# Weight gradient matmuls between the output gradient steps of chunk 1, gradient loads in two parts, and a home of its own for the second half of the attention rows

## The chip, the cores and the metric

The kernel runs on one core of a Trainium2 chip, in one launch. The metric is the device time in microseconds, the median of several runs. A core has TensorE (PE in the profile; its weight loads stand as PEld), VectorE (DVE), ScalarE (ACT), GpSimd (POOL) and SyncE (SP). All five run their own instruction streams in order and meet through semaphores. Transfers run on 16 DMA engines; this kernel issues them from three places: SP (queue q1 in the profile), ACT (q10) and POOL (q0, which has the indirect gathers too).

## The reference: what is computed

One transformer block, forward and backward: the output `h2` and the gradients with respect to the input and six of the weights.

```python
def _A_ref(x, wqkv, wo):            # B, S, D = 1, 2048, 512; H = 32; Dh = 16; W, dil = 8, 2
    ...                             # q, k, v = x @ wqkv, by head
    off = jnp.arange(W) * dil       # each position sees itself and 7 earlier ones, 2 apart
    ...
    attn = _softmax(logits, axis=-1)
    o = jnp.einsum("bhsw,bhswd->bhsd", attn, vg)
    return (...)(o, 0, 2, 1, 3).reshape(B, S, D) @ wo

def _B_ref(x, w1, b1, w2, b2):      # F = 1792
    h = _gelu(jnp.einsum("bsd,df->bsf", x, w1) + b1)
    return jnp.einsum("bsf,fd->bsd", h, w2) + b2

h = x + _A_ref(_layernorm(x, axis=-1), A_wqkv, A_wo)
h2 = h + _B_ref(_layernorm(h, axis=-1), B_w1, B_b1, B_w2, B_b2)
...
_out, _vjp = jax.vjp(_f, A_x, A_wqkv, A_wo, B_w1, B_b1, B_w2, B_b2)
return (_out0, *[jnp.asarray(_g) for _g in _vjp(grad_out)])
```

All arrays are bf16. The attention has no matmul form of the usual kind: each query has eight keys, so its products are made on VectorE over gathered rows and summed on TensorE with small constant matrices.

## The kernel before

The 2048 tokens are worked in four chunks of 512 (`NC = 4`), each of four tiles of 128 tokens. There are three parts in time.

1. Forward attention for all chunks, and the second layer norm.
2. Forward and backward MLP by chunk. It writes the activations and their gradients, turned into rows of tokens, to two DRAM tensors: `gT_d` (gelu output) and `ghT_d` (gradient before gelu). `gh_all[c]` is the gradient with respect to `h`. The loads of the output gradient (`gout_r`, two tiles of 1 MB) for part three are issued from ACT here. A scheduler sets the order of parts one and two.
3. Backward attention. From `tc.manual_schedule()` (L817) on, every engine has its instructions in exactly the order in which the Python code emits them.

In part three two strands are woven together by hand. The **main strand** loops over the chunks (L1100). For chunk `c` it makes the softmax gradient (`ga_prod` on DVE, L656; `ga_sum` on PE, L662), and then three kinds of "band": for the gradients of q (chunk `c`), of v and of k (chunk `c-1`). A band (`band_tile`, L1004) takes a tile of gathered rows `R` (an indirect gather from POOL, L224), multiplies it on DVE by coefficients (`prb`, L1012), sums on PE (`ps_band`, L1026), is copied by ACT to `gqs` or `gks` (L1029) and stored by POOL to the DRAM tensors `g3_d` (`gq_d`, `gk_d`, `gv_d`, L1031). `p3_go(c)` (L1040) makes the gradient of the attention output of chunk `c` in four steps: `a` transposes `gh_all[c]` (L162, copied by ACT at L163 to `ghT`), two steps `b` multiply it by `woT` (L646, copied at L647 to `got`, through one PSUM tile `psL` with a single buffer), and `t` turns it into rows (L210), which ACT copies (`tmst`, L213) and SP stores to `go_d` (L215, L219). The gathers for the v bands read `go_d`.

The **filler strand** is the weight gradients, a generator `wgrads()` (L891): seven pairs of columns for `w2` (`ps_gw`, L896), seven for `w1` (L904), then `wo` (L914) and `wqkv` in the order q, v, k (L924). One matmul is 128x512 wide (128x256 for `w1`). Results leave PSUM through a two-bank pool `psF`, an ACT copy to `gwst` (L831) and a store from ACT (L833).

Work that is due later stands in a list `pend` with the number of slots until then (`later`, L968); `slot(dve_us)` (L971) emits what is due, and then fills with filler matmuls up to `RATIO = 1.4` times the DVE time given, less the PE time just emitted. `filler(us)` (L947) adds its argument to a running debt and draws matmuls, each paid with its cost (`MM = 0.22`), while the debt is positive; a generator can also yield a letter, a gate, at which it stops until the main strand has opened it.

Just ahead of the loop, chunk 1's output gradient is made in one go:

```python
    load_ln1(0)
    load_R()
    load_R()
    p3_go(1, (1, 1, 1, 1))
    slot(0.0)
```

Loads of the filler strand are issued from SP, in the order in which the code emits them, among the main strand's stores. `load_t` (L751) brings one pair of columns of `gT_d` or `ghT_d` (`gwm`, 1 MB, 8 KB in a row per partition) into one of two homes; the load for pair `q + 2` is emitted when pair `q` is done. `load_half` (L738) brings half of the 2048 token rows of a tensor (1 MB, rows of 1 KB) into one of three homes (`rtile`, L734): two are old weight tiles, the third (`r8`, k = 2) is shared by the first half of the layer norm rows `ln2_r` and the second half of the attention rows `o_r`, whose load therefore waits until the first half of the last `w1` pair is computed. `load_g3` (L850) brings one half (1 MB) of `g3_d` into `gqh`. `load_perm` (L841) brings the `ln1_r` rows in eight small loads. SP stands still at a load whose home is not free, and everything emitted behind it stands too.

`shift` (L1058) copies coefficients between partitions: four ACT copies (`sh`, L1062), each emitted after a number of slots given by `at`; the k and v bands need all four (through a DVE transpose to `cf`, L246).

Of the kernel before, what the change touches and what calls it, by code (L numbers as in the profile page):

```python
# [10 lines left out]
P = 128  # L11
BF16 = mybir.dt.bfloat16
# [24 lines left out]
def kernel(  # L37
# [21 lines left out]
    V, A, T, G, SY = nc.vector, nc.scalar, nc.tensor, nc.gpsimd, nc.sync  # L59
# [4 lines left out]
    S, D = xf.shape  # L64
# [3 lines left out]
    NC = S // CH  # L68
# [224 lines left out]
    wff = LP("wff")  # L293
# [444 lines left out]
    def load_half(name, src, i, k, eng=None):  # L738
        r = rtile(name, k)
        n = NT // 2  # L740
        (eng or SY).dma_start(out=r[:], in_=src[i * n * P:(i + 1) * n * P, :].rearrange("(t p) d -> p t d", p=P))
        return r

    ngm = [0]
# [5 lines left out]

    def load_t(src, q, eng=None):  # L751
        t_ = mtile("gwm", [P, 2, NT, P])
        (eng or SY).dma_start(out=t_[:].rearrange("p a t f -> p (a t f)"),
                              in_=src[:, 2 * q:2 * q + 2].rearrange("p a c n -> p (a c n)"))
        return t_

    gout_r = []
# [66 lines left out]
    HN = NT // 2  # L824
    MM = 0.22

    def wg_sink(dst_ap, width=D):
        st = pt3("gwst")

        def sink(o, ps):  # L830
            A.copy(out=st[:, o, :], in_=ps[:])  # L831
            if sink.n:
                A.dma_start(out=dst_ap, in_=st[:].rearrange("p a (b d) -> p (a b) d", d=width))  # L833
            sink.n += 1
        sink.n = 0
        return sink

    def wrows(dst, r0, n, c0, width):
        return dst[r0:r0 + n * P, c0:c0 + width].rearrange("(a p) d -> p a d", p=P)

    def load_perm(name, src, i, k):  # L841
        r = rtile(name, k)
        for j in range(4):
            for m in range(2):
                r0 = i * HN * P + 4 * m + j
                SY.dma_start(out=r[32 * j:32 * j + 32].rearrange("p (s m) d -> p s m d", m=2)[:, :, m, :],
                             in_=_ap(src[r0:r0 + 1, :], [[8 * D, 32], [256 * D, HN // 2], [1, D]]))
        return r

    def load_g3(sel, i):  # L850
        if sel == 2:
            t_ = pt3("rows", "gqh")[:, 0:HN, :]
        else:
            t_ = mtile("gqh", [P, HN, D])
        SY.dma_start(out=t_[:], in_=g3_d[sel][:, i * HN:(i + 1) * HN, :])
        return t_

    def mm_pair(name, mm, cost, sink, sub=1, by_half=False, mid=None):
# [31 lines left out]

    def wgrads():  # L891
        ln2_r = [load_half("ln2_r", ln2_d, 0, 2)]
        o_r = []
        for q in range(7):
            g_ = tiles[q]
            yield from mm_pair("ps_gw2", lambda ps, o, u, i, t, k: T.matmul(ps[:], lhsT=g_[:, o, i * HN + t, :], rhs=gout_r[i][:, t, :], **k), MM,  # L896
                               wg_sink(wrows(out_6, 2 * q * P, 2, 0, D)), by_half=(q == 6),
                               mid=(lambda: ln2_r.append(load_half("ln2_r", ln2_d, 1, 0))) if q == 6 else None)
            n = q + 2
            tiles.append(load_t(gT_d, n) if n < 7 else load_t(ghT_d, n - 7))  # L900
        o_r.append(load_half("o_r", o_d, 0, 1))
        for q in range(7):
            g_ = tiles[7 + q]
            yield from mm_pair("ps_gw1", lambda ps, o, u, i, t, k: T.matmul(  # L904
                ps[:, 256 * u:256 * u + 256].rearrange("p (a f) -> p a f", a=2),
                lhsT=ln2_r[i][:, t, (2 * o + u) * P:(2 * o + u + 1) * P], rhs=g_[:, :, i * HN + t, :], **k), MM / 2,
                wg_sink(wrows(out_4, 0, 4, q * 256, 256), 256), sub=2, by_half=q in (0, 6),
                mid=(lambda: o_r.append(load_half("o_r", o_d, 1, 2))) if q == 6 else None)
            if q + 2 < 7:
                tiles.append(load_t(ghT_d, q + 2))  # L910
        want.append(("q", 0))
        ln1_r = [load_perm("ln1_r", ln1_d, 0, 0)]
        for k2 in range(2):
            yield from mm_pair("ps_gwo", lambda ps, o, u, i, t, k: T.matmul(  # L914
                ps[:], lhsT=o_r[i][:, t, (2 * k2 + o) * P:(2 * k2 + o + 1) * P],
                rhs=gh_all[(i * HN + t) // TPC][:, (i * HN + t) % TPC, :], **k), MM,
                wg_sink(wrows(out_3, 2 * k2 * P, 2, 0, D)), by_half=True,
                mid=(lambda: ln1_r.append(load_perm("ln1_r", ln1_d, 1, 1))) if k2 == 1 else None)
        for si, sel in enumerate((0, 2, 1)):
            yield "qvk"[si]  # L920
            if sel not in hv:
                fetch(sel)
            for d2 in range(2):
                yield from mm_pair("ps_gwq", lambda ps, o, u, i, t, k: T.matmul(  # L924
                    ps[:], lhsT=ln1_r[i][:, t, (2 * d2 + o) * P:(2 * d2 + o + 1) * P], rhs=hv[sel][i][:, t, :], **k), MM,
                    wg_sink(wrows(out_2, 2 * d2 * P, 2, sel * D, D)), by_half=(si == 0 and d2 == 0))
            if sel == 0:
                want.append(("k", 1))

    hv = {}  # L930
    want = [("v", 2)]
# [39 lines left out]
    def slot(dve_us):  # L971
        pe = 0.0
        for x in list(pend):
            x[0] -= 1
            if x[0] <= 0:
                pend.remove(x)
                x[2]()
                pe += x[1]
        filler(dve_us * RATIO - pe)
# [60 lines left out]
    def p3_go(c, at=(1, 2, 3, 4)):  # L1040
        ghT = pt3("ghT")
        got = pt3("got")
        st3[c]["got"] = got

        def a():
            to_fm(gh_all[c], ghT)

        def b(g0):
            def f():
                go_pair(g0, ghT, got)  # L1050
            return f

        def t():
            to_tm_store(p3, got, 0, go_d, c, False, stage=lambda: pt3("tmst"))
        for n, cost, f in zip(at, (1.0, 1.8, 1.8, 1.0), (a, b(0), b(2), t)):
            later(n, cost, f)

    def shift(c, src, at):  # L1058
        sh = pt3("sh")

        def cp(w4):
            A.copy(out=sh[32 * w4:32 * w4 + 32],  # L1062
                   in_=_sub(src[32 * w4:32 * w4 + 32, 0, 0:1], [[SP + 2, 2], [1, 512]], c * CH + 4 * w4))
        for w4 in range(4):
            later(at[w4], 0.0, lambda w4=w4: cp(w4))
        return sh
# [28 lines left out]
    load_ln1(0)  # L1095
    load_R()
    load_R()
    p3_go(1, (1, 1, 1, 1))
    slot(0.0)
    for c in range(NC + 2):  # L1100
        if 0 < c < NC:
            got, vw = st3[c]["got"], st3[c]["vw"]
# [31 lines left out]
                      lambda gs=gs, sc=sc, c=c: unperm(gs[:], gqkv[c - 1][:, 8:12, :], 4, sc * 256))  # L1134

        if c == NC:
            shk = shift(c - 1, glf, (1, 1, 2, 2))
        if c > 0:
            vtile(0)
            vtile(1)  # L1140
# [7 lines left out]
        if 0 < c < NC:  # L1148
            V.tensor_tensor(out=glf[:, :, c * CH:(c + 1) * CH], in0=L[:], in1=attn_c(c), op=ALU.mult)
            if c == 1:  # L1150
                V.memset(glf[:, :, S:SP], 0.0)
        if c < NC:
            cfq = coefs(pt3, glf[:, 0, 0:1], c * CH, SP)
        if 0 < c < NC:
# [82 lines left out]
```

## Time and profile before

| | before |
|---|---|
| median of 5 runs | 668.12 us (665.82 to 671.17) |
| the profiled execution: its time | 666.55 us |
| its span, first to last instruction | 664.4 us |
| PE busy in the span | 597.0 us, 90% |
| DVE busy | 517.3 us, 78% |
| ACT busy | 375.9 us, 57% |
| POOL busy | 149.5 us, 22% |
| moved by DMA | 158.98 MB, 239 GB/s in the mean |
| part three, first transposes for chunk 1 | at 377.9 us |

Busy time is the union of an engine's instructions. Times in the views are from the start of the span. In a timeline row the bracket tells how long the engine stood idle before the row, and whose end released it; in the rows of windows the columns are the stretch, its length, the busy time of PE, PEld, DVE, ACT and POOL (instructions in brackets), the granted TensorE clock as a share of full speed, the DMA engines' busy share, and GB/s.

### The profile page before, as it was taken

To read this page: it belongs to the slowest core of one execution; us is meant where nothing else is said; L and a number is where in the kernel's file an instruction comes from. 1 tells how busy PE (TensorE), PEld (TensorE's weight loads), DVE (VectorE), ACT (ScalarE), POOL (GpSimd) and SP (SyncE) were. 2 spreads that over 40 slices of the span, in tenths; PEclk is the share of its full clock that TensorE was granted. 3 is DMA by queue.
4 is the path that set the end of the run, shared out by engine and by line. 5 is a ranking of instruction groups with operands and counts; after the bars stand their busy time and mean duration, and the time that the engine had idled before them with its cause. 6 is when DMAs were issued, how large, how long until landed. Compare 5 with 4: busy or idle time off the path is not lost. (4 is left out here: it accounts for less than half of the span.)

```text
span 664.4 us, 10165 instructions
## 1 busy us (share of the span) xinstructions
PE 597.0 (90%) x3854; PEld 290.1 (44%) x3916; DVE 517.3 (78%) x760; ACT 375.9 (57%) x601; POOL 149.5 (22%) x183
## 2 busy tenths in 40 slices
PE   3888989697699899999999979989999999979897
PEld 1443434332344344444444433434566667434343
DVE  7989979868899668888849768867977789569230
ACT  2587877688684567377351353684368337455321
POOL 3341535431101111110110222221232023112010
PEclk9999999898899989999999989999999999999999
DMA  8583849744999995987995999887797679997621
GB/s 277 172 290 119 294 146 299 245 137 96 218 224 254 229 259 126 239 237 170 252 279 165 282 330 343 340 275 286 238 396 287 247 231 340 356 308 255 210 77 47
DMA packets 147947, 158.98 MB, mean 239 GB/s; under 512 B 94476, under 2 KB 132540, under 8 KB 141244
## 3 DMA queue, kind: packets, MB, share of 16 engines
q1 hardware_dynamic: 120076, 69.58, 41.4%
q0 software_dynamic: 15376, 77.63, 33.7%
q10 hardware_dynamic: 12448, 11.14, 5.3%
q8 instruction: 30, 0.49, 0.3%
q14 instruction: 17, 0.14, 0.1%
HBM read 87.76 MB, written 48.03 MB: 204 GB/s over the span
## 5 line engine op out<-in xcount | busy, mean ns | idle before, releaser
L1012 DVE TENSOR_TENSOR prb<-R,cf 128x2048 bf16<-128x2048 bf16 x96 | 111.5, 1220 | 28.5 <-PE ps_band L1026 21.6
L184 ACT ACTIVATE gyr<-ps_gl,rstd 128x512 bf16<-128x512 f32 x32 | 22.0, 687 | 86.1 <-PE ps_gl L636 48.8
L577 PE MATMUL ps_h<-ln2T,w 128*128 128x512 bf16 x217 | 56.7, 386 | 3.8 <-ACT xa L579 3.1
L610 PE MATMUL ps_f<-w,gt 128*128 128x512 bf16 x219 | 53.4, 393 | 4.2 <-DVE gt L585 3.9
L896 PE MATMUL ps_gw<-gout_r,gwm 128*128 128x512 bf16 x216 | 51.8, 385 | 3.2 <-DMA gwm<-gT_d 2.2
L622 PE MATMUL ps_gg<-goT,w2T 128*128 128x512 bf16 x220 | 54.1, 378 | 0.4
L904 PE MATMUL ps_gw<-gwm,ln_r 128*128 128x256 bf16 x448 | 52.9, 273 | 0.7 <-ACT gwst L831 0.7
L636 PE MATMUL ps_gl<-w1T,dt 128*128 128x512 bf16 x219 | 51.7, 379 | 0.8 <-ACT gyr L184 0.4
L924 PE MATMUL ps_gwq<-gqh,ln_r 128*128 128x512 bf16 x186 | 44.2, 386 | 6.3 <-ACT gwst L831 3.7
L341 PE MATMUL ps_qkv<-ln1T,wqkv 128*128 128x512 bf16 x185 | 46.9, 392 | 1.0 <-DMA go_d<-zrow 0.6
L656 DVE TENSOR_TENSOR pr<-got,vw 128x4096 bf16<-128x4096 bf16 x16 | 36.2, 2287 | 14.9 <-ACT got L653 9.7
L904 PEld LDWEIGHTS <-ln_r 128*128 128x128 bf16 x448 | 43.0, 98 | 9.2 <-issue 3.0
L578 ACT ACTIVATE xb<-ps_h,b1c 128x512 bf16<-128x512 f32 x56 | 38.3, 693 | 12.0 <-DVE xa L589 6.5
L624 DVE CUSTOM_DVE_ANT_0 dt<-ps_gg,dt 128x512 bf16<-128x512 f32 x56 | 37.6, 685 | 8.5 <-PE ps_gg L622 8.4
L579 ACT ACTIVATE xa<-ps_h,b1c 128x512 bf16<-128x512 f32 x56 | 38.3, 699 | 9.5 <-DVE dt L590 9.5
L562 POOL DMA_DIRECT2D gT_d<-tst x16 | 12.4, 774 | 133.9 <-DMA tst<-gt 132.0
L280 ACT COPY gqkvT<-ptu 128x1024 bf16<-128x1024 bf16 x24 | 24.3, 1011 | 28.9 <-PE ptu L279 28.8
L262 DVE TENSOR_TENSOR prb<-R,cf 128x2048 bf16<-128x2048 bf16 x32 | 37.6, 1210 | 2.9 <-DMA R<-v_d,rowi 1.9
L232 DVE TENSOR_TENSOR pr<-qt,kt 128x4096 bf16<-128x4096 bf16 x16 | 36.1, 2286 | 2.1 <-PE ps_band L267 1.1
L610 PEld LDWEIGHTS <-gt 128*128 128x128 bf16 x224 | 22.5, 101 | 33.0 <-DVE gt L585 4.9
L213 ACT COPY tmst<-ptm 128x1024 bf16<-128x1024 bf16 x32 | 31.3, 1022 | 6.4 <-PE ptm L210 3.7
L636 PEld LDWEIGHTS <-dt 128*128 128x128 bf16 x224 | 21.4, 98 | 29.0 <-DVE gb1p L624 2.4
(182 smaller groups left out, 1130.0 us busy)
## 6 DMA issues: line engine op xcount, KB each, us to landing
gwm<-ghT_d SPq DMA_DIRECT2D x7, 1024.0 KB
gT_d<-tst POOLq DMA_DIRECT2D x12, 512.0 KB
ghT_d<-tst POOLq DMA_DIRECT2D x12, 512.0 KB
gwm<-gT_d SPq DMA_DIRECT2D x6, 1024.0 KB
out_dram<-gwst ACTq DMA_DIRECT2D x22, 256.0 KB
ln_d<-ln POOLq DMA_DIRECT2D x8, 512.0 KB
vw<-vf_d SPq DMA_DIRECT2D x4, 528.0 KB
xt<-in_A_x_dram SPq DMA_DIRECT2D x4, 512.0 KB
```

Source lines behind the costliest of these rows:

```text
L262: V.tensor_tensor(out=pr[:, hf].rearrange("p j (d h) -> p j d h", h=H), in0=R[:, o:o + 4, :].rearrange("p j (d h) -> p j d h", h=H), in1=c ...
L341: T.matmul(ps[:], lhsT=wqkv[:, dc, sel * D + g * P:sel * D + (g + 1) * P], rhs=st_[c]["ln1T"][:, dc, :], start=(dc == 0), stop=(dc == DC - 1))
L577: T.matmul(ps[:], lhsT=wcol(w1, dc, f), rhs=ln2T[c][:, dc, :], start=(dc == 0), stop=(dc == DC - 1))
L578: A.activation(out=xb[:, f - f0, :], in_=ps[:], func=ACT.Identity, bias=b1c[:, f:f + 1])
L579: A.activation(out=x2[:, f - f0, :], in_=ps[:], func=ACT.Square, bias=b1c[:, f:f + 1])
L610: T.matmul(ps[:], lhsT=gts[f // 4][:, f % 4, j * P:(j + 1) * P], rhs=wrow(w2, f), start=(f == 0), stop=False)
L622: T.matmul(ps[:], lhsT=wcol(w2T, dc, f), rhs=goT[:, dc, :], start=(dc == 0), stop=(dc == DC - 1))
L636: T.matmul(ps[:], lhsT=dts[f // 4][:, f % 4, j * P:(j + 1) * P], rhs=wrow(w1T, f), start=(f == 0), stop=(f == FT - 1))
L896: yield from mm_pair("ps_gw2", lambda ps, o, u, i, t, k: T.matmul(ps[:], lhsT=g_[:, o, i * HN + t, :], rhs=gout_r[i][:, t, :], **k), MM, w ...
L904: yield from mm_pair("ps_gw1", lambda ps, o, u, i, t, k: T.matmul(ps[:, 256 * u:256 * u + 256].rearrange("p (a f) -> p a f", a=2), lhsT=ln ...
L924: yield from mm_pair("ps_gwq", lambda ps, o, u, i, t, k: T.matmul(ps[:], lhsT=ln1_r[i][:, t, (2 * d2 + o) * P:(2 * d2 + o + 1) * P], rhs=h ...
L1012: V.tensor_tensor(out=pr[:, 4 * hf:4 * hf + 4].rearrange("p j (d h) -> p j d h", h=H), in0=R[:, o:o + 4, :].rearrange("p j (d h) -> p j d ...
```

## The change

- `p3_go(1, ...)`: the four steps become due in four successive slots, and after each of them 0.5, 0.6, 1.0 and 1.0 us of filler is drawn. The debt that the step itself left is kept and put back, less what was drawn.
- `load_t`, `load_half` and `load_g3` issue two DMAs of 512 KB for each of 1 MB. For `gT_d` the parts are the two columns of the pair (4 KB in a row per partition), for `ghT_d` the two halves of the tokens (2 KB in a row, both columns), for `load_half` and `load_g3` four token tiles each (1 KB and 4 KB in a row).
- The second half of the attention rows gets two new tiles `o_late` in the homes of `ghT` and `got` (`w18`, `w28`), loaded when the last chunk's softmax gradient is emitted, in place of the load into `r8` in the middle of the last `w1` pair. The filler has a gate `"o"` ahead of the `wo` gradient, opened with that load.
- The very last pair of `wqkv` results is stored in two DMAs, one after each ACT copy (`apart`).
- The `shift` of the last chunk's k coefficients is spread over slots (1, 2, 3, 3) in place of (1, 1, 2, 2).

In the order of instructions, DVE and POOL are unchanged. On PE, 16 matmuls of the first `w2` pair move ahead: 3 after the transposes, 3 between the two `woT` steps, 5 before the row transposes and 5 after them, where 6 stood after; the run of 27 behind the first q band becomes 17. After that PE's order is the same to the end. On SP, the load of `ln2_r` moves from behind the stores of chunk 1's `go_d` rows to ahead of them. On ACT, one of the last chunk's four `sh` copies moves from ahead of the `wo` results' copies to behind the next transposed copy. Semaphores are kept for each part of a load: PE waits for the first part before the first matmul that reads it, and for the second before the first that reads that.

```diff
     def load_half(name, src, i, k, eng=None):
         r = rtile(name, k)
         n = NT // 2
-        (eng or SY).dma_start(out=r[:], in_=src[i * n * P:(i + 1) * n * P, :].rearrange("(t p) d -> p t d", p=P))
+        for k_ in range(0, n, n // 2):
+            r0 = (i * n + k_) * P
+            (eng or SY).dma_start(out=r[:, k_:k_ + n // 2, :], in_=src[r0:r0 + n // 2 * P, :].rearrange("(t p) d -> p t d", p=P))
         return r
...
     def load_t(src, q, eng=None):
         t_ = mtile("gwm", [P, 2, NT, P])
-        (eng or SY).dma_start(out=t_[:].rearrange("p a t f -> p (a t f)"),
-                              in_=src[:, 2 * q:2 * q + 2].rearrange("p a c n -> p (a c n)"))
+        for o in range(2):
+            if src is gT_d:
+                (eng or SY).dma_start(out=t_[:, o].rearrange("p t f -> p (t f)"), in_=src[:, 2 * q + o].rearrange("p c n -> p (c n)"))
+            else:
+                (eng or SY).dma_start(out=t_[:, :, 8 * o:8 * o + 8, :].rearrange("p a t f -> p a (t f)"),
+                                      in_=src[:, 2 * q:2 * q + 2, 2 * o:2 * o + 2].rearrange("p a c n -> p a (c n)"))
         return t_
...
             A.copy(out=st[:, o, :], in_=ps[:])
-            if sink.n:
+            if apart:
+                A.dma_start(out=dst_ap[:, o:o + 1, :], in_=st[:, o:o + 1, :])
+            elif sink.n:
                 A.dma_start(out=dst_ap, in_=st[:].rearrange("p a (b d) -> p (a b) d", d=width))
...
-        SY.dma_start(out=t_[:], in_=g3_d[sel][:, i * HN:(i + 1) * HN, :])
+        for k_ in range(0, HN, 4):
+            SY.dma_start(out=t_[:, k_:k_ + 4, :], in_=g3_d[sel][:, i * HN + k_:i * HN + k_ + 4, :])
...
-                mid=(lambda: o_r.append(load_half("o_r", o_d, 1, 2))) if q == 6 else None)
+                mid=None)
...
+        yield "o"
         for k2 in range(2):
             yield from mm_pair("ps_gwo", lambda ps, o, u, i, t, k: T.matmul(
-                ps[:], lhsT=o_r[i][:, t, (2 * k2 + o) * P:(2 * k2 + o + 1) * P],
+                ps[:], lhsT=(o_r[0][:, t] if i == 0 else o_late[t // 4][:, t % 4])[:, (2 * k2 + o) * P:(2 * k2 + o + 1) * P],
...
+    def load_o_late():
+        for k, tag in enumerate(("w18", "w28")):
+            t_ = wff.tile([P, 4, D], BF16, name="o_late", tag=tag, bufs=1)
+            SY.dma_start(out=t_[:], in_=o_d[(HN + 4 * k) * P:(HN + 4 * k + 4) * P, :].rearrange("(t p) d -> p t d", p=P))
+            o_late.append(t_)
+        open_gates.add("o")
...
-    p3_go(1, (1, 1, 1, 1))
-    slot(0.0)
+    p3_go(1, (1, 2, 3, 4))
+    for us in (0.5, 0.6, 1.0, 1.0):
+        slot(0.0)
+        owed, fs["debt"] = fs["debt"], 0.0
+        filler(us)
+        fs["debt"] += owed - us
...
         if c == NC:
-            shk = shift(c - 1, glf, (1, 1, 2, 2))
+            shk = shift(c - 1, glf, (1, 2, 3, 3))
...
+            if c == NC - 1:
+                load_o_late()
```

More of the change, by code (lines that the diff above doesn't have):

```diff
@@ L825, with wg_sink @@
     MM = 0.22
-    def wg_sink(dst_ap, width=D):
+    def wg_sink(dst_ap, width=D, apart=False):
         st = pt3("gwst")
@@ L925, in wgrads @@
                     ps[:], lhsT=ln1_r[i][:, t, (2 * d2 + o) * P:(2 * d2 + o + 1) * P], rhs=hv[sel][i][:, t, :], **k), MM,
-                    wg_sink(wrows(out_2, 2 * d2 * P, 2, sel * D, D)), by_half=(si == 0 and d2 == 0))
+                    wg_sink(wrows(out_2, 2 * d2 * P, 2, sel * D, D), apart=(si == 2 and d2 == 1)), by_half=(si == 0 and d2 == 0))
             if sel == 0:
                 want.append(("k", 1))
+    o_late = []
+    def load_o_late():
[4 more added lines that the diff above has]
+        open_gates.add("o")
     hv = {}
```

## The prediction

> **What bounds the kernel now.** I read the page first, then the stretches of part three with the granted clock, then PE's timeline for its idle gaps, and at each gap the timeline of what released it.
>
> ```profile
> PE 597.0 (90%) x3854; PEld 290.1 (44%) x3916; DVE 517.3 (78%) x760; ACT 375.9 (57%) x601; POOL 149.5 (22%) x183
> PE ps_gwq L924 4%; PE ps_gl L1082 2%; DMA gv_d<-gks 1%; DMA gqh<-gv_d 1%; DVE prb L1012 1%; POOL R L224 0%; DVE u L192 0%; ACT gks L1029 0%; DVE u L195 0%; DVE u L194 0%; ACT gwst L831 0%; PE ps_band L1026 0%; PE ptu L279 0%; POOL gv_d L1031 0%; POOL out_dram L1087 0%
> ```
>
> PE is busy 90% of the span, and the chain that ended last is PE matmuls, with two transfers in it (the store and reload of the v gradient). The gain to be had is PE's idle time, so the next view is the stretches.
>
> ```profile
> 378.00:388.00 10.00, 6.56 (x52) 3.71 (x52) 2.54 (x7) 5.52 (x8) 1.29 (x2) 1.00 1.01 373
> 388.00:394.00 6.00, 3.36 (x22) 1.13 (x22) 6.00 (x6) 4.29 (x6) 0.42 (x1) 0.84 0.85 278
> 394.00:400.00 6.00, 6.00 (x25) 2.43 (x23) 5.05 (x4) 1.66 (x3) 3.97 (x3) 0.88 0.95 332
> 400.00:440.00 40.00, 38.44 (x297) 17.28 (x301) 34.69 (x28) 23.73 (x31) 10.20 (x8) 1.00 0.87 316
> 593.00:600.00 7.00, 3.27 (x18) 1.70 (x15) 6.71 (x12) 5.47 (x9) 0.56 (x1) 0.77 0.88 313
> ```
>
> PE loses time at 378 to 400 and at 593 to 600, and there the clock falls too; between, from 400 to 440, it is nearly full. PE's timeline names the gaps:
>
> ```profile
> 381.06 1.45 PE L646 MATMUL ps_go<-ghT,woT 128*128 128x512 bf16 x6 [0.63 <-ACT ghT L163]
> 383.61 1.89 PE L646 MATMUL ps_go<-ghT,woT 128*128 128x512 bf16 x8 [1.10 <-ACT got L647]
> 386.60 0.96 PE L210 MATMUL ptm<-Pmat,got 128*128 128x128 bf16 x14 [0.99 <-ACT got L647]
> 390.09 0.40 PE L1026 MATMUL ps_band<-prb,S 128*32 128x512 bf16 x4 [0.73 <-DVE prb L1012]
> 447.45 1.04 PE L896 MATMUL ps_gw<-gout_r,gwm 128*128 128x512 bf16 x4 [2.24 <-DMA gwm<-gT_d]
> 597.28 1.01 PE L924 MATMUL ps_gwq<-gqh,ln_r 128*128 128x512 bf16 x2 [3.73 <-ACT gwst L831]
> 621.66 1.89 PE L924 MATMUL ps_gwq<-gqh,ln_r 128*128 128x512 bf16 x8 [2.18 <-DMA gqh<-gv_d]
> ```
>
> Four places, and each is touched by a part of the change. After 621.66 nothing but PE's own work stands before the end.
>
> **Part by part.** A 128x512 matmul costs 0.216 us start to start (four of them take from 581.71 to 582.57). Sums are made against the profiled execution, 666.55 us; the median of the runs is 1.6 us above it.
>
> *Output gradient of chunk 1.* No work is added. Ten more filler matmuls than before (16, not 6) stand ahead of the first q band. Their places are 3 (0.65 us) in the idle time before 381.06 (0.42 + 0.30 + 0.63), 3 (0.65) in the 1.10, 5 (1.08) in the 0.99, and 5 where 6 ran. ACT's copies stay the chain. The band's end, 393.0, is set by DVE:
>
> ```profile
> 387.67 9.17 DVE L1012 TENSOR_TENSOR prb<-R,cf 128x2048 bf16<-128x2048 bf16 x8 [6.20 <-DMA R<-k_d,rowi]
> 400.75 2.29 DVE L656 TENSOR_TENSOR pr<-got,vw 128x4096 bf16<-128x4096 bf16 x1 [1.70 <-PE ps_band L1026]
> ```
>
> So the run behind the band shrinks from 27 to 17 and the next band comes 10 x 0.216 = 2.2 us earlier; its products are done at 396.8, before its new time of 397.9. DVE's 1.70 us wait was for that band, so it can follow. If the clock no longer falls, the six matmuls at half speed (0.43 apart) gain 1.3 more. The lower bound is -0.4: SP now issues the 1 MB `ln2_r` load ahead of the `go_d` stores, while the gather `R` is moving, which has no slack; at 0.4 MB/us it could cost 2.6. But the queues' counts at 385 to 387 have q0 at 0.74 MB against 0.09 on q1 with 1 KB rows already waiting: such rows hardly slow the gather. I take 2.2.
>
> The `go_d` stores then wait behind that 1 MB, some 3.6 us, so the gathers that POOL issued at 393.58 and 395.69 go out near 397 and 399, and POOL's `gq_d` store and `R<-k_d` gather stand behind. The v band needs its rows at 409.5 (407.3 shifted), and they took 10 us for both: covered by some 3 us for the first gather, more for the second.
>
> *`gT_d` in two columns.* The 2.24 us at 447.45 is a load issued at 439.25, held on SP behind a `go_d` store. In 441 to 444 q1 moved 0.85 MB of it, the rest crawled beside a gather. The first column (0.52 MB) is thus in at about 443, and PE wants it at 445.2. The second is wanted 16 matmuls and a band later, at 449.6; its tail may land as late. Between 0 and 2.24, I take 1.9.
>
> *`gqh` in four-tile parts.* At 621.66 PE waited for 1 MB issued at 616.27, when the last `gv_d` store had landed. Only the last 512 KB depends on that store; at 617 to 620 q1 moved 0.16, 0.24 and 0.36 MB, so it is in near 620, and PE wants it four matmuls after 619.5, at 620.3. Between 0 and 2.18, I take 1.9.
>
> *`shift` (1, 2, 3, 3).* ACT's order at 594 explains the longest gap:
>
> ```profile
> 594.52 2.09 ACT L1062 COPY sh<-glf 32x1024 bf16<-32x1024 bf16 x2
> 596.64 1.07 ACT L831 CAST gwst<-ps_gwo 128x512 bf16<-128x512 f32 x2
> ```
>
> One of the two `sh` copies (1.04 us) goes behind; `gwst` starts 1.04 earlier and so does PE. Three copies then stand ahead of the band's copies: about 0.6 us later on ACT at 602.7, which delays a store, not PE. DVE's transpose of all four waits until 605.7, and they are done at 602.3. [...] I take 1.7. DVE, full here (6.71 of 7), lets PE come about 2.5 earlier at most.
>
> *`o_late`.* SP no longer stands 14.1 us at the `o_r` load (waits of the SP queue: L741 behind `ps_gw` L904); it goes out near 546 and not 559.5, PE wants it at 569. The gate is open before the filler reaches it, as PE's order is unchanged. No PE wait hung on it: 0. If that cover were gone, PE would wait for 1 MB, 3 us.
>
> *The last store in two.* After the last copy 128 KB and not 256 KB are left; at 662 0.26 MB moved in 1 us. Between 0.1 and 0.5, I take 0.3.
>
> *Costs.* SP issues 23 more DMAs of 0.33 us, covered, since SP mostly stands waiting. ACT issues two more `gout_r` parts; one now stands between `h2s` and the first `ghT` copy at 344, where PE waited 0.27 and 0.31 us for ACT: 0.4. The other extra issues on ACT lie in idle time. Finer rows in transfer: 0.2. Between 0 and 1.2, I take 0.6.
>
> Sum: 2.2 + 1.9 + 1.9 + 1.7 + 0.3 - 0.6 = 7.4. 666.55 - 7.4 = 659.2 for a profiled execution, 660.7 for the median.
>
> [...] By the rows, most loads find q0 empty (507 to 511: q1 1.03 MB, q0 0.01). [...]
>
> **Rivals.**
>
> [...]
>
> *DVE becomes the pacer from 400.* It is busy 34.7 of 40 us there. Then the first two gains (4.1) are lost: 664.8. Against: in part three it waited 26.8 us for `ps_band`, so it has reserve; 1.70 of it by 401 against the 2.2 asked.
>
> *The `ln2_r` load delays the first gather* by its full 2.6 us: 663.3.
>
> *It does not do what it says:* the parts land together, since one queue serves both, and `sh` only changes places with another wait. The waits stay: about 667.6.
>
> **How the numbers follow.** Main case 0.64, likely within 657.5 and 664; DVE 0.14; `ln2_r` 0.09; starved 0.09; nothing 0.04. Half a per cent is 3.3 us, about what a measurement here can tell from no change: the bound is 664.8, and the DVE case lies on it, so half counts as faster. Faster 0.64 + 0.07 + 0.09 = 0.80, same 0.11, slower 0.09. The range runs from 656.5 (all upper bounds together are 11.1, which gives 657.0) to 667.5, leaving out the starved and the empty case.
>
> **What would show it.** Right: gaps at 381 to 387 filled with L896; 17 matmuls behind the first band; no `gwm<-gT_d` wait near 443; the gap ahead of L924 near 2.7 us and the clock there above 0.9; no `gqh<-gv_d` wait over 0.5. Wrong: PE idle released by `gwm<-ghT_d` (starved), DVE's wait for `R<-k_d` above 6.2 (`ln2_r`), `ps_band` waiting for `prb` past 400 (DVE).

## The result and the profile after

The changed kernel takes 663.86 us (median of 42 runs, 656.2 to 668.65) against 668.66 us for the kernel before (79 runs): ratio 0.995, 95% interval [0.9929, 0.9971], a gain of some 3.3 us where 7.4 were forecast. Ratios here compare the undisturbed runs of both kernels, so they can differ a little from the ratio of the medians. Timed twice more, on other occasions, it gave 1.0005 [0.9971, 1.0038] and 0.9882 [0.9841, 0.9924]: its executions differ much more than the first interval tells. The profiled execution took 667.01 us, near the upper end of the runs.

The first line has the engines' sums, the next ones the stretches of part three (columns as before).

```profile
PE 597.0 (90%) x3854; PEld 289.5 (44%) x3916; DVE 517.4 (78%) x760; ACT 375.5 (56%) x601; POOL 155.3 (23%) x183
```

```profile
378.00:388.00 10.00, 8.85 (x63) 4.79 (x63) 2.98 (x7) 4.95 (x8) 2.62 (x3) 1.00 0.99 363
388.00:394.00 6.00, 3.54 (x28) 1.35 (x27) 5.99 (x6) 5.11 (x7) 0.00 (x0) 1.00 1.04 368
394.00:400.00 6.00, 6.00 (x40) 2.30 (x38) 6.00 (x5) 3.97 (x6) 2.50 (x1) 1.00 0.61 168
400.00:440.00 40.00, 34.70 (x242) 15.28 (x247) 30.58 (x26) 17.73 (x23) 15.91 (x10) 0.91 0.85 314
593.00:600.00 7.00, 4.46 (x31) 2.27 (x29) 6.73 (x10) 4.93 (x9) 1.57 (x2) 0.92 0.81 260
```

Up to 400 it went as forecast: PE 8.85 of 10 us busy instead of 6.56, clock 1.00. Then 400 to 440, the fullest stretch before, has lost 3.7 us of PE time and the clock has fallen to 0.91; DMA moves 168 GB/s in 394 to 400, where it moved 332. PE's timeline at the four places:

```profile
381.62 1.46 PE L646 MATMUL ps_go<-ghT,woT 128*128 128x512 bf16 x6 [0.22 <-ACT ghT L163]
384.18 1.89 PE L646 MATMUL ps_go<-ghT,woT 128*128 128x512 bf16 x8 [0.45 <-ACT got L647]
416.11 0.40 PE L1045 MATMUL ps_band<-prb,S 128*32 128x512 bf16 x4 [1.06 <-DVE prb L1031]
449.40 1.04 PE L905 MATMUL ps_gw<-gout_r,gwm 128*128 128x512 bf16 x4 [0.75 <-DMA gwm<-gT_d]
597.76 0.59 PE L934 MATMUL ps_gwq<-gqh,ln_r 128*128 128x512 bf16 x2 [2.54 <-ACT gwst L837]
622.99 1.02 PE L934 MATMUL ps_gwq<-gqh,ln_r 128*128 128x512 bf16 x4 [1.92 <-DMA gqh<-gv_d]
```

The gaps of the output gradient are nearly filled, the `gT_d` wait went from 2.24 to 0.75, the shift's gap from 3.73 to 2.54; the `gqh` wait stayed (1.92, forecast under 0.5). New is 416.11: PE waits for the v band's products. DVE and POOL tell why:

```profile
397.10 8.89 DVE L656 TENSOR_TENSOR pr<-got,vw 128x4096 bf16<-128x4096 bf16 x4
414.83 2.36 DVE L1031 TENSOR_TENSOR prb<-R,cf 128x2048 bf16<-128x2048 bf16 x2 [6.89 <-DMA R<-go_d,rowi]
```

```profile
397.50 9.32 POOL L224 DMA_INDIRECT R<-go_d,rowi  x1 [16.26 <-issue]
407.12 0.94 POOL L224 DMA_INDIRECT R<-go_d,rowi  x1 [0.30 <-issue]
```

Before, the same two instructions of POOL read:

```profile
393.58 1.81 POOL L224 DMA_INDIRECT R<-go_d,rowi  x1 [13.68 <-DMA go_d<-tmst]
395.69 1.97 POOL L224 DMA_INDIRECT R<-go_d,rowi  x1 [0.31 <-issue]
```

The gather is issued 3.9 us later, as the prediction said (the `go_d` stores lie behind the 1 MB `ln2_r` load). But then POOL is busy with it for 9.32 us, until DVE's four products are over (397.10 + 8.89 = 405.99), DVE waits 6.89 us for the band's rows, and PE goes idle behind it.

### The profile page after: what moved, and what is told of

Same layout as the page of the kernel before. It is cut to its first block, busy times and chain, and to the rows that moved or that the text cites. A ratio compares the mean times of both kernels' runs of the same rounds, so it can differ in the third digit from the quotient of the medians.

```text
span 664.7 us, 10206 instructions
## 1 busy us (share of the span) xinstructions
PE 597.0 (90%) x3854; PEld 289.5 (44%) x3916; DVE 517.4 (78%) x760; ACT 375.5 (56%) x601; POOL 155.3 (23%) x183
```

## The experiments

Times of single runs of one kernel spread over some 12 to 25 us, so a profile's own stages tell more than medians of a few us apart; but each row below is one execution. Two lengths are read from each profile: A, from chunk 1's first transpose (the first `pt<-ident,gh` row of PE in part three) to the last chunk's first v product (DVE's `prb` row, at 592.50 before and 594.17 after), and B, from there to the end of the span. The output gradient steps and the `gT_d` columns act in A; the shift, the `gqh` parts and the last store in B. "Gather" is POOL's time in the first `R<-go_d`, and "ends" how many ends of DVE instructions passed in it.

| kernel | gather us | ends | A us | B us | ratio to before (95%) |
|---|---|---|---|---|---|
| before | 1.81 | 1 | 214.38 | 71.86 | |
| changed | 9.32 | 4 | 215.48 | 70.54 | 0.995 [0.9929, 0.9971] |
| a_again | 9.77 | 5 | 211.83 | 70.74 | 1.0005 [0.9971, 1.0038] |
| a_third | 10.39 | 5 | 216.22 | 72.28 | 0.9882 [0.9841, 0.9924] |
| a_lnr_late | 1.92 | 1 | 216.29 | 72.06 | 0.9962 [0.9931, 0.9994] |
| a_lnr_q5 | 1.49 | 1 | 211.17 | 70.82 | 0.995 [0.9918, 0.9981] |
| a_prod_halves | 1.28 | 1 | 207.90 | 71.86 | none (6 runs) |
| a_halves_2 | 0.96 | 1 | 209.98 | 72.02 | 0.9949 [0.9918, 0.9981] |
| a_halves_gv | 9.84 | 8 | 215.49 | 70.25 | 0.9939 [0.9898, 0.9979] |
| a_gqh_whole | 9.85 | 5 | 215.50 | 73.15 | 0.9998 [0.9961, 1.0035] |
| a_gv_act | 9.71 | 5 | 214.18 | 71.02 | 0.9951 [0.9919, 0.9983] |
| a_cf_early | 1.06 | 1 | 210.56 | 72.19 | 0.9894 [0.9837, 0.9951] |
| a_cf_early_2 | 2.71 | 1 | 209.20 | 70.70 | none (1 run) |
| a_cf_early_3 | 2.80 | 1 | 210.41 | 71.45 | 0.9884 [0.9822, 0.9945] |
| b_lnr_early | 3.41 | 2 | 214.10 | 71.86 | 0.9985 [0.9959, 1.0011] |
| b_lnr_q5 | 6.20 | 4 | 214.14 | 72.00 | 1.0028 [0.9998, 1.0058] |
| b_steps_lnr | 1.61 | 1 | 216.02 | 71.47 | 1.0001 [0.9968, 1.0033] |
| b_steps_q5 | 12.69 | 7 | 217.40 | 71.57 | 1.001 [0.9972, 1.0049] |
| b_shift | 1.58 | 1 | 214.40 | 74.84 | 1.0006 [0.9977, 1.0036] |
| b_cf_early | 5.57 | 4 | 218.47 | 71.67 | 1.0023 [0.9994, 1.0051] |

Kernels named a_ start from the changed kernel, b_ from the one before.

**Is it the load's place?** First the changed kernel once more, then it with the load behind the third `gT_d` load, the old kernel with only the load moved ahead, and the old kernel with only the steps.

```diff
 # a_lnr_late, in wgrads
-        ln2_r = [load_half("ln2_r", ln2_d, 0, 2)]
+        ln2_r = []
...
             tiles.append(load_t(gT_d, n) if n < 7 else load_t(ghT_d, n - 7))
+            if q == 0:
+                ln2_r.append(load_half("ln2_r", ln2_d, 0, 2))
 # b_lnr_early
+    lnr0 = load_half("ln2_r", ln2_d, 0, 2)
     p3_go(1, (1, 1, 1, 1))
 # b_steps_lnr: p3_go(1, (1, 2, 3, 4)) and its four slots, with a_lnr_late's edit
```

> The changed kernel once more. Theory (the 1 MB ln2_r load, now ahead of chunk 1's go_d stores on SP, delays the rows' gathers into DVE's block of ga_prod products): the first R<-go_d gather is again issued near 397.5 and lasts about 9 us, DVE's prb again waits 5 to 7 us for it; time about 663.5, 0.993 to 0.997 of before. Rival (an accident of that one execution): the gather lasts about 2 us here and the wait is under 1 us, with the time the same as in the first runs.

> The changed kernel with the ln2_r load issued behind the third gT_d load, so that the go_d stores land before it. Theory: the gather goes out near 394 and lasts 1.8 to 2 us, DVE's wait for R<-go_d falls from 6.9 to under 1 us, the clock stays over 0.97 in 400 to 440, and part three is 4 to 6 us shorter than in the changed kernel (ratio to before about 0.988). Rival, packet sizes (finer rows in the split loads cost what is missing): within 1 us of the changed kernel. Rival, DVE as pacer (DVE has no reserve behind 400, so that work moved forward on PE gains nothing): within 1 us of the changed kernel, with ps_band waiting for prb past 400 as before.

> The kernel before, with only the ln2_r load moved ahead of chunk 1's output gradient steps; nothing else of the change. Theory: 3 to 5 us slower than before (ratio 1.004 to 1.008), with the first R<-go_d gather out near 397 instead of 393.6 and lasting into DVE's products. Rivals, packet sizes and DVE as pacer: no difference from before beyond 1 us.

> The kernel before, with only the output gradient steps spread over the slots (1, 2, 3, 4) and the weight gradient matmuls between them, and the ln2_r load kept behind the go_d stores. Theory: 2 to 3.5 us faster than before (ratio 0.995 to 0.997), clock 1.00 in 388 to 400, the second q band some 2 to 3 us earlier, gather as in before. Rival, packet sizes: the same gain, since no load is split here. Rival, DVE as pacer: no gain beyond 1 us.

The long gather came again (9.77 us, DVE's wait 4.70); the ratio did not (1.0005). With the load late the gather took 1.92 us and DVE waited for no `R<-go_d`, as the theory said; yet A was no shorter (216.29). PE now ran into the next thing, the `gT_d` rows of pair q = 2, which it wanted earlier and which shared the queue with the moved load. PE's timeline of a_lnr_late, and of b_steps_lnr, which gained nothing either (1.0001, A 216.02):

```profile
404.11 0.60 PE L905 MATMUL ps_gw<-gout_r,gwm 128*128 128x512 bf16 x2 [0.50 <-DMA gwm<-gT_d]
418.43 2.27 PE L905 MATMUL ps_gw<-gout_r,gwm 128*128 128x512 bf16 x6 [3.10 <-DMA gwm<-gT_d]
```

```profile
409.99 0.61 PE L896 MATMUL ps_gw<-gout_r,gwm 128*128 128x512 bf16 x2 [2.28 <-DMA gwm<-gT_d]
450.22 1.04 PE L896 MATMUL ps_gw<-gout_r,gwm 128*128 128x512 bf16 x4 [2.43 <-DMA gwm<-gT_d]
```

And b_lnr_early refuted the simple form of the theory: with the load ahead and the gather late, the old kernel lost nothing (A 214.10, forecast 3 to 5 us slower). Its gather took 3.41 us. So the late issue alone cost nothing there.

**The load out of the stretch, and shorter products.** In a_lnr_q5, b_lnr_q5 and b_steps_q5 the load goes behind pair q = 5 (`if q == 5:` in the edit above). In a_prod_halves each of chunk 1's products is two instructions of half the size:

```diff
-        V.tensor_tensor(out=pr, in0=got[:, g, :].unsqueeze(1).to_broadcast([P, W, 512]),
+        for w0 in range(0, W, W // 2) if halves else (0,):
+            n = W // 2 if halves else W
+            V.tensor_tensor(out=pr[:, w0:w0 + n], in0=got[:, g, :].unsqueeze(1).to_broadcast([P, n, 512]),
...
```

> The changed kernel with the first ln2_r load (1 MB) put off until the weight gradient pair q = 5, some 80 us into part three. Part three is counted from the first transpose of chunk 1's gradient (it took 286.2 us before, 286.0 and 282.6 in two profiles of the changed kernel, 288.4 with the load one pair back). Theory (the stretch behind the output gradient steps is bound by transfers: the 1 MB is too much there wherever it stands): gather near 11 us after the start as with the load one pair back, and now no wait for gwm<-gT_d over 1 us in the first 60 us (it was 0.50 and 3.10); part three 279 to 282 us, 4 to 6 less than before; ratio 0.990 to 0.993. Rival (only the place of the gathers counts): as with the load one pair back, gT_d waits of some 3 us, part three about 287. Rival (the load is missed later): PE waits for ln_r at the first ps_gw1 pair by over 2 us, which takes the gain back.

> The kernel before, with only the ln2_r load put off until pair q = 5. Theory of the transfers: the old order has its gaps on PE anyway (3 us up to 388), the gT_d loads come sooner but are asked for late: 0 to 2 us shorter than before, part three 284 to 286; the clock dips at 388 to 400 as before. Rival (the place of the load was all that was wrong with the stretch): 3 us or more shorter. Rival (only the place of the gathers counts): no change, within 0.5 us.

> The kernel before with the output gradient steps spread and filled with weight gradient matmuls, and the ln2_r load put off until pair q = 5; no load is split. Theory of the transfers: 2.5 to 4 us shorter than before in part three (282 to 284), 1 to 2 less gain than the changed kernel with the same load put off, which has the shift and the split loads as well. Rival (the steps bring nothing, DVE or PE's own work sets the pace): as the kernel before with the load alone put off. Rival (only the gathers' place counts): as with the load one pair back, about 287.5, with gT_d waits over 2 us.

> The changed kernel with chunk 1's products pr (L656) made in halves: eight tensor_tensor of 128x2048 in place of four of 128x4096, the same work, with the ln2_r load left ahead of the go_d stores. Theory (the gather's descriptors wait for a pause between DVE's instructions, and the long products give few): the first R<-go_d gather, 9.3 and 9.8 us long in the changed kernel, takes 2 to 4 us, DVE's wait for it falls to 2 us or less. Rival (it waits for the whole block of products, whose instructions follow without a pause): it again ends 0.8 us after the last product, 9 to 10 us long. Rival (it waits for the DMA queue, not for DVE): its length is unchanged while its end does not stand at 0.8 us after a DVE instruction.

a_lnr_q5 did what the theory of transfers asked (no `gT_d` wait over 0.30 us before 440, A + B 282.0) and the load was not missed later; its ratio, 0.995, is that of the changed kernel. But b_steps_q5 had the gather shut out for 12.69 us, though it was issued at 390.83, among the band's products of 1.2 us each: it is not the load's place that decides. In b_lnr_q5 it was shut out for 6.20 us, and A was as before, since it had been issued early. In a_prod_halves the gather was in after 1.28 us and A the shortest of all. That looked like a cure.

**Again, and the tail.** a_halves_2 repeats it; a_halves_gv adds ACT as issuer of the last `gv_d` stores; a_gv_act has that alone; a_gqh_whole undoes the `gqh` parts.

```diff
 # a_gqh_whole
-        for k_ in range(0, HN, 4):
-            SY.dma_start(out=t_[:, k_:k_ + 4, :], in_=g3_d[sel][:, i * HN + k_:i * HN + k_ + 4, :])
+        SY.dma_start(out=t_[:], in_=g3_d[sel][:, i * HN:(i + 1) * HN, :])
 # a_gv_act
-                G.dma_start(out=g3_d[sel]...
+                (A if kind == "v" and c == NC - 1 else G).dma_start(out=g3_d[sel]...
```

> The changed kernel with the gqh loads whole again (1 MB each), all else as changed. Theory (the last gv_d store, behind the gathers on POOL's queue, sets when the last gqh rows can be asked for: 23.4 to 23.9 us after the last chunk's first v product in three of four profiles of the changed kernel, as before; 22.3 where the store was issued 1.7 earlier): the load is again issued near 23.8, and PE waits for it 0 to 1.5 us longer than the changed kernel's 1.9 to 2.3. Rival, from the prediction (the size of what depends on the store counts for its full 1.9): the wait is 1.9 us longer than with the two parts. Rival (the two parts hurt, since two stores are waited for one after the other and finer rows move slower): the wait falls to 0.5 to 1.5 us and the end comes 1 to 2 us earlier.

> The changed kernel with the last chunk's two gv_d stores issued by ACT, each behind the copies that fill it, in place of POOL; all else as changed. Theory (on POOL's queue they stand behind the R<-q_d gather): the second store lands 2 to 4 us after its issue and not 6.4 to 7, the last gqh load goes out 2.5 to 4 us earlier, PE's wait for gqh falls from 1.9 to 2.3 us to under 0.5, and the time from the last chunk's first v product to the end falls from 70.5 to 70.8 us to 68 to 69. Rival (the transfers of that stretch are full anyway, whichever queue): landing and wait within 0.5 us of the changed kernel's. Rival (the issue on ACT delays the copies behind it): the next gks copies 0.5 us later, the end no earlier.

> The changed kernel with chunk 1's products in halves and the last chunk's gv_d stores issued by ACT. Theory (two separate losses, the gather shut out by the long products and the store behind the gathers): the gains add: part three 277 to 279 us against 286.2 before and 279.8 with the halves alone; ratio to before 0.983 to 0.990, faster than both kernels. Rival (one gives way to the other, since PE's progress is given back at the next transfer): part three no shorter than 279.5.

> The changed kernel with chunk 1's products in halves, the kernel of the earlier look run again. Theory (instructions of 1.2 us give a gather a place to get in, those of 2.3 us often don't): the first R<-go_d gather takes 2 to 3.5 us again, DVE does not wait for it over 1 us, part three 279 to 283 us by whether the clock falls near 13 us; ratio to before 0.988 to 0.994. Rival (the short gather was luck, since gathers are let in at random in both forms): the gather takes 4 us or more again and part three is 284 or more.

In a_prod_halves and a_halves_2 the gather was issued during the last band product and got in at that product's end, before the first short product had run: neither tested the short products on it. a_halves_gv did, and there the cure fell; its edit of the stores lies 200 us behind this place. DVE and POOL there:

```profile
396.61 9.17 DVE L658 TENSOR_TENSOR pr<-got,vw 128x2048 bf16<-128x2048 bf16 x8
405.69 2.02 DVE L246 STREAM_TRANSPOSE cf<-sh 128x1024 bf16<-128x1024 bf16 x1
415.21 3.50 DVE L1033 TENSOR_TENSOR prb<-R,cf 128x2048 bf16<-128x2048 bf16 x3 [7.50 <-DMA R<-go_d,rowi]
```

```profile
396.76 9.84 POOL L224 DMA_INDIRECT R<-go_d,rowi  x1 [16.58 <-issue]
406.90 0.94 POOL L224 DMA_INDIRECT R<-go_d,rowi  x1 [0.30 <-issue]
```

Eight short products went by; the gather ended at 406.60, 0.82 us after the last of them (405.78), when the transpose was running. The second, issued while the transpose ran, took 0.94.

In the tail, ACT as issuer changed nothing: the last `gqh` load went out 23.55 us into B (23.90 in the changed kernel, 23.42 in a_again) although the store was issued 6.85 us ahead of it on a queue of its own; the wait was 2.52 us. That is what the rival had forecast; full transfers as the reason fit (DMA share 0.91 in those 6.85 us) but are not shown. With whole `gqh` loads PE waited 3.30 us and B was 73.15, against 70.25 to 72.28 in the twelve profiles of the changed order with the two parts.

**A transpose as a door.** Moving DVE's transpose of the v coefficients between the first and second product changes no other engine's order:

```diff
             for g in range(4):
+                if c == 1 and g == 1:
+                    cfv = coefs(pt3, st3[0]["sh"][:, 0, 0:1], 0, 512)
                 pr = pt3("prod", "pr")
...
-            cfv = coefs(pt3, st3[c - 1]["sh"][:, 0, 0:1], 0, 512)
+            if c != 1:
+                cfv = coefs(pt3, st3[c - 1]["sh"][:, 0, 0:1], 0, 512)
```

> The changed kernel with DVE's transpose of the v coefficients (L246, 2.0 us) moved from behind chunk 1's four products to behind the first of them; nothing else differs on any engine. In all four profiles so far with whole products and the early ln2_r load the first R<-go_d gather took 9.3 to 9.9 us and ended at the same point, 0.8 us after the last product, when this transpose began; gathers issued while a transpose runs took 1.0 us. Theory (a transpose lets the gather's descriptors through, products do not): the gather ends 1 us or less into the moved transpose, 2 to 4 us after its issue, DVE's wait for R<-go_d is under 1.5 us, and part three is 3 to 5 us shorter than with the gather shut out (279 to 283 against 285.2 to 288.7). Rival (the gather waits for something outside DVE, which comes at that time by itself): it takes 9 to 10 us again. Rival (random): either, and different in the second look.

> The kernel with the transpose moved, a second look. Theory: again 2 to 4 us. Rival (random, as with the products in halves, where it took 1.3, 1.0 and 9.8): 9 us or more in one of the two.

> The kernel before with the shift of the last chunk alone at (1, 2, 3, 3). Theory (the transfers that bring the last v gradient back set the end of part three, and PE's gain is given back there): the gap ahead of the second ps_gwq pair falls from 3.73 to 2.54 us, and PE waits as much longer for gqh, so that the time from the last chunk's first v product to the end stays at 71.5 to 72.0 us. Rival, from the prediction (1.7 us gained and kept): that time falls to 69.8 to 70.5.

> The kernel with the transpose moved, timed again beside the changed kernel and beside the kernel before with the same move. Theory (the shut-out gather is what kept the change from its forecast gain): ratio to before 0.986 to 0.992, gather 1 to 4 us. Rival (the first timing, of six runs, was luck): 0.994 to 0.998.

> The changed kernel, a third time. Theory: ratio to before 0.994 to 1.000, some 4 us above the kernel with the transpose moved on the same chip; the gather again 9 to 10 us long. Rival (random): a gather of 1 to 3 us and part three near 281.

> The kernel before, with only the transpose moved behind the first product. Theory (before, the gather comes earlier, beside the band's products, and is let in there as a rule: it took 1.5 to 1.9 us in four of six profiles with this place, 6.2 and 12.7 in two): 0 to 2 us faster than before, the gather under 3 us. Rival (the gain of the moved transpose has nothing to do with the changed kernel's order): 4 us or more faster than before, as in the changed kernel.

In three profiles the gather took 1.06, 2.71 and 2.80 us and DVE did not wait for its rows. Only in a_cf_early_2 was the transpose itself the door. In a_cf_early the gather was in before it, at the end of the last band product, and in a_cf_early_3 it got in at a pause of 1.04 us, in which DVE waited for ACT's `sh` copies ahead of the moved transpose. DVE, then POOL of a_cf_early_2:

```profile
395.63 2.28 DVE L656 TENSOR_TENSOR pr<-got,vw 128x4096 bf16<-128x4096 bf16 x1
397.83 2.02 DVE L246 STREAM_TRANSPOSE cf<-sh 128x1024 bf16<-128x1024 bf16 x1
399.77 6.65 DVE L656 TENSOR_TENSOR pr<-got,vw 128x4096 bf16<-128x4096 bf16 x3
406.35 2.35 DVE L1031 TENSOR_TENSOR prb<-R,cf 128x2048 bf16<-128x2048 bf16 x2
```

```profile
396.01 2.71 POOL L224 DMA_INDIRECT R<-go_d,rowi  x1 [16.14 <-issue]
399.03 0.94 POOL L224 DMA_INDIRECT R<-go_d,rowi  x1 [0.30 <-issue]
```

And of a_cf_early:

```profile
391.01 9.38 DVE L1031 TENSOR_TENSOR prb<-R,cf 128x2048 bf16<-128x2048 bf16 x8 [5.87 <-DMA R<-k_d,rowi]
400.31 2.28 DVE L656 TENSOR_TENSOR pr<-got,vw 128x4096 bf16<-128x4096 bf16 x1
```

```profile
400.15 1.06 POOL L224 DMA_INDIRECT R<-go_d,rowi  x1 [16.04 <-issue]
```

The same stretches, ahead of and behind 409, of the changed kernel and of a_cf_early_2:

```profile
396.00:409.00 13.00, 12.84 (x87) 4.87 (x86) 11.95 (x7) 3.88 (x6) 11.20 (x4) 1.00 0.50 146
409.00:425.00 16.00, 12.16 (x70) 4.94 (x71) 10.17 (x9) 4.18 (x6) 2.83 (x4) 0.79 1.02 382
```

```profile
396.00:409.00 13.00, 12.59 (x86) 4.67 (x79) 13.00 (x8) 3.30 (x5) 6.27 (x5) 1.00 0.99 364
409.00:425.00 16.00, 15.47 (x123) 7.57 (x122) 15.70 (x16) 9.70 (x14) 3.14 (x4) 1.00 1.03 412
```

With the gather shut out DMA stands half idle for 13 us (share 0.50) and the work is missing behind (PE 12.16 of 16 us busy); with the gather in it is full throughout (0.99, then 1.03).

This kernel's two timings, 659.67 us (0.9894) and 660.86 us (0.9884), six runs each, lie near the lowest ratios of the study. Against the changed kernel the times do not show a gain: timed beside a_cf_early_3, that kernel reached 0.9882 (median 661.96, forecast some 4 us above), its runs going from 651.9 to 673.8, and the profiled one, among its slowest, was again shut out (10.39). Its short runs may be those in which the gather got in; no profile shows one of them. In b_cf_early the move brought nothing (1.0023, A 218.47): its gather came at 390.26, among the band's products, and was let in at the pause behind the first product, 5.57 us later. That pause, 3.10 us, was DVE's wait for ACT's `sh` copies, which the moved transpose now wanted too early.

b_shift undid the other half of the forecast:

```profile
590.60 0.59 PE L924 MATMUL ps_gwq<-gqh,ln_r 128*128 128x512 bf16 x2 [2.54 <-ACT gwst L831]
616.68 3.57 PE L924 MATMUL ps_gwq<-gqh,ln_r 128*128 128x512 bf16 x8 [3.65 <-DMA gqh<-gv_d]
```

```profile
615.00:621.00 6.00, 4.32 (x16) 1.31 (x19) 0.00 (x0) 0.00 (x0) 0.00 (x0) 0.51 0.68 276
```

The gap shrank from 3.73 to 2.54 us, and PE then stood 3.65 us, not 2.18, at the next transfer, behind which the clock fell to half. B became 3.0 us longer in this profile.

## Why the prediction was right or wrong

**The output gradient steps and the `gT_d` columns: the step that failed is "covered".** Take A where the gather was let in early in the changed order: 207.90, 209.98, 210.56, 209.20 and 210.41, mean 209.6 (the two with halves, the three with the transpose moved). Four profiles with the old order and no edit that acts in A (before, b_lnr_early, b_lnr_q5, b_shift) give 214.38, 214.10, 214.14, 214.40, mean 214.3. That is 4.6 us; the prediction had 2.2 + 1.9 = 4.1. Where the gather was shut out in the changed order (the changed kernel, a_again, a_third, a_gqh_whole, a_gv_act, a_halves_gv) the mean is 214.8, from 211.83 to 216.22: on the mean the gain and 0.5 more are gone. The prediction saw that the stores would lie behind the `ln2_r` load and that the gathers would go out near 397, and then wrote that this was "covered by some 3 us for the first gather". It compared issue times, with the gather's 1.81 us of before carried over. The term measured 9.3 to 10.4 us in all five profiles of the changed order with whole products and the transpose in its old place. What it did not ask is what DVE would be doing at the gather's new time.

Two limits stand. By these profiles part three, A + B, takes 286.1 us on the mean of the six shut out, as in the old order (286.1 in before, b_lnr_early and b_lnr_q5), and 281.3 in the five let in; the median's gain of 3.3 us lies between, as a mixture of both would, but no profile of the changed kernel itself has the gather let in. And the two gains were seen only together: the steps without the columns (b_steps_lnr, b_steps_q5) had A at 216.02 and 217.40, with PE standing at whole `gT_d` loads for 4.7 us.

**Is the early load to blame?** It moves the gather into the products, or to the last 0.1 to 0.8 us ahead of them, and there it was shut out in five of five. But it is not needed (b_steps_q5, 12.69 us; b_lnr_q5, 6.20) and not enough (b_lnr_early, 3.41). Late, the load's megabyte brings waits for `gT_d` (3.10 us in a_lnr_late) instead: the stretch there, 402 to 422, runs at a DMA share of 0.98 to 1.08.

**The `gT_d` columns by themselves** held. PE's wait near 70 us into part three was 2.24, 2.45, 2.43, 2.78, 2.49, 2.74 and 4.73 us with whole `gT_d` loads (before, b_lnr_early, b_steps_lnr, b_lnr_q5, b_shift, b_cf_early, b_steps_q5), and 0 to 1.15 with the columns.

**The clock** was not counted as a gain up to 400, rightly: 13 to 19 us into part three it fell to about half for 3.4 us in some profiles and not in others with the same order of PE (0.84 in 388 to 394 before, 1.00 in the same place in b_lnr_early; 1.00 changed, 0.81 in a_again). Filling the gaps did not decide it. For the shift the prediction did count it: of its 1.7 us only the 1.04 by which `gwst` starts earlier are read from a row; the other 0.7, for a clock that stays up behind the shorter gap, were the author's estimate, and no run shows this term. In the kernel before, the clock stood at 0.50 from 597 to 600, behind the idle 3.73 us, and at 1.00 behind 2.24 and 2.18; but it fell to 0.50 at 393 to 395 too, behind gaps of 0.73 and 0.74. With the shift the gap measured 2.54 us, and behind it the clock fell in eight of the fourteen profiles that have this gap (0.80 over 594.17 to 602.17 in the changed kernel) and held in six. So the 0.7 could not be counted on.

**The `gqh` parts, the shift and the last store** were forecast at 1.9 + 1.7 + 0.3 = 3.9 us in B and brought 0.4: B is 71.9 in before, b_lnr_early and b_lnr_q5, and 71.5 on the mean of the eight of the changed order with the `gqh` parts and POOL's stores (changed, a_again, a_third, a_halves_2, a_prod_halves and the three with the transpose moved). The shift's gap fell by 1.19 in all profiles that have it. But PE ends its last wait for `gqh<-gv_d` 28.6 to 29.7 us into B in all 20 profiles, with the shift or without it, with whole loads or parts: the time of that landing decides, and PE that comes sooner waits longer. The prediction had the last 512 KB in near 620, 3.7 us behind an issue at 616.27; it took 4.9 in the changed kernel (issued 23.90 us into B, PE went on at 28.82), hardly less than the whole 1 MB before (5.4). Behind that wait 42.7 us are left in the old order and 41.6 to 41.7 in the changed one, where the clock held: this 1.0 is what the parts and the store bring, 0.86 from four matmuls that no longer stand behind the wait, 0.12 from the last store (3.09 to 2.97 us from the last copy to the end). The failed step is the sum across one chain: the shift's gain and the parts' gain end at the same landing, and neither moved it.

The rest of the difference is the clock. In a_cf_early it stayed at 1.00 behind the shift's gap, and the end came 1.5 us later than in a_cf_early_2, where it fell:

```profile
592.12:600.12 8.00, 5.46 (x49) 2.69 (x48) 7.68 (x13) 7.07 (x11) 0.69 (x2) 1.00 0.67 229
620.12:626.12 6.00, 4.51 (x30) 1.55 (x30) 0.00 (x0) 1.35 (x3) 0.52 (x1) 0.72 0.63 250
```

```profile
586.52:594.52 8.00, 5.46 (x30) 2.64 (x29) 7.68 (x13) 6.94 (x11) 0.69 (x2) 0.79 0.67 222
614.52:620.52 6.00, 4.48 (x37) 2.01 (x37) 0.00 (x0) 2.10 (x3) 0.54 (x1) 1.00 0.88 345
```

PE that came sooner waited longer for `gqh` (0.64 + 2.51 us, not 2.10) and lost the clock there. The twelve profiles of the changed order with parts split this way: in six the clock fell behind the shift's gap and held behind the `gqh` wait (B 70.25 to 71.02), in six the other way round (B 71.45 to 72.28).

**The rivals.** Starved `ghT_d` loads, the 0.09 among the chances: PE waits for none of them in any profile. DVE as pacer: its sign came (`ps_band` waiting for `prb` at 416.11), but DVE had run on from 388.01 without a wait and itself stood 6.89 us for the gather, so no. Parts that land together: not for `gT_d` (2.24 to 0.75 us); for `gqh` and the shift this rival was close, as told above. The `ln2_r` load delaying the `R<-k_d` gather: DVE's wait for it was 5.74, before 6.20; no. **The costs** were of the forecast kind: PE's wait for the first `ghT` copy in part two rose from 0.31 to 0.87 us, 0.56 for the 0.4 forecast (0.6 to 0.9 in the other profiles of the changed order). The 0.2 for finer rows was the author's estimate, and no run shows it; what was measured is that the last 512 KB of `gqh` took 4.9 us, the whole 1 MB before 5.4.

**Left open:** why a gather sometimes gets in at the first end of a DVE instruction and sometimes at none until a transpose or a pause, and in what share of executions; whether moving the transpose makes the changed kernel faster; what decides where the clock falls; and which transfer exactly holds back the last `gv_d` store.

## What to carry to other kernels

When a change moves a gather of GpSimd's queue, ask what VectorE does at its new time, since the trace of the old place says nothing on it (here 1.81 us before, 9.32 after); where VectorE runs two-input products back to back, a pause or another instruction close behind the gather's issue (here a transpose, seen to work in one profile, where the gather took 2.71 us) is worth a trial. Before adding up the gains of parts that stand ahead of the same transfer, ask whether its landing moves: here it did not, and 3.9 us of forecast gains brought 0.4. And when single runs of a kernel spread widely, look in several profiles for an event that happens in some of them, before explaining a median.

## What the hardware showed that was not expected

In all 20 profiles the first `R<-go_d` gather ended 0.81 to 0.82 us after the end of a DVE instruction, 0.96 to 12.69 us after its start. In ten it was the first end that came; in the other ten two to eight ends passed, and all ten got in where DVE either paused (0.24 us was enough, in b_lnr_early and b_lnr_q5) or began a transpose. In all gathers of part three, in these profiles, the same is seen: of 260 issued during a band product or a softmax gradient product, both of whose inputs are in SBUF, 250 were in by the second end. Nine of the other ten are this first `R<-go_d`, so the shut-out is rare elsewhere. And each of the 62 that passed an end coming 0.1 us or more after its issue got in at a pause or a transpose. The 89 gathers issued while a transpose ran took 0.94 to 1.01 us, and the 78 issued during products with one input in PSUM (`pp` and `glf`) 0.96 to 1.00.

Why it is so is not shown. What is shown is that the gather's end follows DVE's instructions, and that the products with one input in PSUM held none of 78 gathers up (0.96 to 1.00 us). A wait for nothing but the end of the instruction that runs would be over within 2.3 us, the length of one product (2.28 us at 396.76 before); up to eight ends were passed over, so such a wait is not the whole of it.
